# First queries over the two hardware DMA queues, and a score tile moved ahead of a token product, in a fused attention and mixer kernel

## The chip, the cores and the metric

One core of one Trainium2 chip. The time is that of the whole program on the device, in microseconds (us), as the median of several executions; lower is better. A profile is one of these executions with every instruction recorded.

## The reference

Attention with a squared ReLU, then a mixer over tokens and channels:

```python
scores = q @ k.transpose / sqrt(64)              # 8 batches, 12 heads, 448 tokens, 64 wide
attn = maximum(scores, 0) ** 2 / 448
x = attn @ v                                      # heads joined: (8, 448, 768)
h = maximum(x.T @ w_tok1, 0) @ w_tok2             # over tokens, 256 hidden
u = x + h.T
out = u + maximum(u @ w_ch1, 0) @ w_ch2           # over channels, 1536 hidden
```

Inputs and output are fp32; the kernel works in bf16 with fp32 sums.

## The kernel before

Work goes in steps of four heads (24 steps). The first keys come in fp32 over the two hardware queues (issued by the sync engine and by ScalarE) and are cast on chip; everything else is loaded by GpSimd, whose transfers cast on their way. PSUM is the memory into which PE, the matrix engine, writes its results; SBUF holds the operands. Tiles that the profile names: `xT` is a step's attention output, `x_sb` the same turned for the token product, `r_sb` the ReLU of a product, `uT` (`uT_sb`) the sum u.

```python
k_first = consts.tile([128, 2, QC, D], FP32, name="k_first")
def load_four(i, names="qkv"):
    for name in names:
        t = raw.tile([128, 2, QC, D], BF16, name=f"{name}_raw")
        for r in range(2):                                   # two heads on 64 partitions each
            eng, dst = nc.gpsimd, t
            if i == 0 and name == "k":
                eng, dst = (nc.sync, nc.scalar)[r], k_first
            eng.dma_start(...)
        if i == 0 and name == "k":
            nc.scalar.copy(t[:, 0], k_first[:, 0])           # the cast, half each
            nc.vector.tensor_copy(t[:, 1], k_first[:, 1])
        raws[i, name] = t
# ... (cut)
def transposes_first():
    for w, dst in ((1, keys), (0, queries)):                 # keys first
        # 28 matmuls that transpose raws[0, "qk"[w]] into PSUM (cut)
        if w:
            nc.scalar.copy(...); nc.vector.tensor_copy(...)  # keys to SBUF
        else:
            nc.vector.tensor_copy(...)                       # queries to SBUF
# ... (cut)
def scores(i, c, alone=False):
    ps = ps_att.tile([128, 2, 512], FP32, tag="att", name="sc_ps")   # two such buffers
    # 4 matmuls, then ReLU on ScalarE (on VectorE where alone); squares follow on VectorE (cut)
# ... (cut)
load_four(0, "kqv"); load_four(1, "qk"); load_wt1(); load_four(2, "qk")
load_four(1, "v"); load_wt2()
# ... (cut)
keep_clock(2, warm_ps)          # matmuls on zeros, whose result is not used
transposes_first()
keep_clock(3, warm_ps)
for i in range(DB):             # the first three steps
    for c in range(QC):         # seven score tiles
        scores(i, c, alone=(i, c) == (0, 2))
        # values, token products, transposes of the next step (cut)
        if c == 6:
            values(i, (0, 1))
            if i > 0:
                token1(i - 1)
```

Of the kernel before, what the change touches and what calls it, by code (L numbers as in the profile page):

```python
# [9 lines left out]
FP32 = mybir.dt.float32  # L10
# [6 lines left out]
def kernel(  # L17
# [11 lines left out]
    nc = tc.nc  # L29

    B, H, S, D = q.shape
# [7 lines left out]
    QC = S // 64  # L39
# [9 lines left out]
    consts = ctx.enter_context(tc.tile_pool(name="consts", bufs=1))  # L49
# [19 lines left out]


    raws = {}
    k_first = consts.tile([128, 2, QC, D], FP32, name="k_first")
    def load_four(i, names="qkv"):
        b, d = divmod(i, DB)
        for name in names:
            src = {"q": q, "k": k, "v": v}[name]
            t = raw.tile([128, 2, QC, D], BF16, name=f"{name}_raw")
            for r in range(2):
                h0 = 4 * d + 2 * r
                eng, dst = nc.gpsimd, t  # L80
                if i == 0 and name == "k":
                    eng, dst = (nc.sync, nc.scalar)[r], k_first
                eng.dma_start(  # L83
                    out=dst[64 * r : 64 * (r + 1)].rearrange("p g c d -> p g (c d)"),
                    in_=src[b, h0 : h0 + 2].rearrange("g (p c) d -> p g (c d)", c=QC),
                )
            if i == 0 and name == "k":
                nc.scalar.copy(t[:, 0], k_first[:, 0])
                nc.vector.tensor_copy(t[:, 1], k_first[:, 1])
            raws[i, name] = t  # L90

    def load_wt1():
        w = moe_w_tok1.rearrange("(p c) j -> c p j", c=QC)
        for c in range(QC):
            r = 64 * (c % 2)
            nc.gpsimd.dma_start(out=wt1[r : r + 64, c // 2, :], in_=w[c])
# [11 lines left out]
    def load_wc1(i, parts):  # L108
        n = DC // parts
        nc.gpsimd.dma_start(  # L110
            out=wc1[:, :, i * n : (i + 1) * n],
            in_=moe_w_ch1.rearrange("(g p) n -> p g n", p=128)[:, :, i * n : (i + 1) * n],
        )
# [44 lines left out]
    def transposes_first():  # L158

        sb = attn.tile([128, 2, 2, S], BF16, name="qkT")  # L160
        qkT[0] = sb
        keys = [ps_acc.tile([128, 1024], BF16, tag=f"acc{r}", name="kT_ps") for r in range(2)]
        queries = ps_att.tile([128, 2, 1024], BF16, tag="att", name="qT_ps")
        for w, dst in ((1, keys), (0, [queries[:, r] for r in range(2)])):
            for c in range(QC):
                for r in range(2):
                    h = slice(64 * r, 64 * (r + 1))
                    for g in range(2):
                        nc.tensor.matmul(
                            dst[r][64 * g : 64 * (g + 1), c * 64 : c * 64 + 64],  # L170
                            lhsT=raws[0, "qk"[w]][h, g, c, :],
                            rhs=ident[h, h],
                            is_transpose=True,
                            start=True,
                            stop=True,
                            skip_group_check=True,
                        )
            if w:
                nc.scalar.copy(sb[:, 0, 1], keys[0][:, :S])
                nc.vector.tensor_copy(sb[:, 1, 1], keys[1][:, :S])  # L180
            else:
                nc.vector.tensor_copy(sb[:, :, 0], queries[:, :, :S])

    def scores(i, c, alone=False):
        sb = qkT[i]
        ps = ps_att.tile([128, 2, 512], FP32, tag="att", name="sc_ps")
        for r in range(2):
            for g in range(2):
                h = slice(64 * g, 64 * (g + 1))
                nc.tensor.matmul(  # L190
                    ps[64 * r : 64 * (r + 1), g, :S],
                    lhsT=sb[h, r, 1, c * 64 : (c + 1) * 64],
                    rhs=sb[h, r, 0, :],
                    start=True,
                    stop=True,
                    skip_group_check=True,
                )
        at = attn.tile([128, 2, S], BF16, name="at", bufs=12)
        if alone:
            nc.vector.tensor_scalar(  # L200
                out=at, in0=ps[:, :, :S], scalar1=0.0, scalar2=None, op0=ALU.max
            )
        else:
            nc.scalar.activation(at, ps[:, :, :S], AF.Relu)  # L204
        squares.append(at)
        at2[i, c] = at

    def square(keep=0):
        while len(squares) > keep:
            at = squares.pop(0)  # L210
            nc.vector.tensor_tensor(out=at, in0=at, in1=at, op=ALU.mult)  # L211

    def values(i, cs):
        v_raw = raws[i, "v"]
        if i not in accs:
            accs[i] = [ps_acc.tile([128, 512], FP32, tag=f"acc{r}", name="acc_ps") for r in range(2)]
        ps = accs[i]
        for c in cs:
            at = at2.pop((i, c))
            for r in range(2):  # L220
                for g in range(2):
                    h = slice(64 * r, 64 * (r + 1))
                    nc.tensor.matmul(  # L223
                        ps[r][64 * g : 64 * (g + 1), :S],
                        lhsT=v_raw[h, g, c, :],
                        rhs=at[h, g, :],
                        start=(c == 0),
                        stop=(c == QC - 1),
                        skip_group_check=True,
                    )  # L230
# [58 lines left out]
    def token1(i):  # L289
        x_sb = x_tiles.pop(i)  # L290
        ps = ps_mm.tile([128, JC, 256], FP32, tag="bank", name="t1_ps")
        for j in range(JC):
            for c in range(4):
                nc.tensor.matmul(  # L294
                    ps[:, j, :],
                    lhsT=wt1[:, c, j * 128 : (j + 1) * 128],
                    rhs=x_sb[:, :, c, :],
                    start=(c == 0),
                    stop=(c == 3),
                )  # L300
        r1 = mix.tile([128, JC, 256], BF16, name="r1_sb")
        nc.scalar.activation(r1, ps, AF.Relu)
        r1_tiles[i] = r1
# [109 lines left out]
    def channel1_begin():  # L413
        r2_tiles[0] = mix.tile([128, EC, 2 * S], BF16, name="r2_sb")
        first = [ps_acc.tile([128, 512], FP32, tag=f"acc{e}", name="m1_ps2") for e in range(2)]
        for e in range(2):
            channel1_part(first, e, range(CC - 2))
        return first
# [122 lines left out]
    def keep_clock(n, warm_ps):  # L541

        for m in range(n):
            for r in range(2):
                h = slice(64 * r, 64 * (r + 1))
                nc.tensor.matmul(
                    warm_ps[h, :], lhsT=warm[h, :64], rhs=warm[h, :],
                    start=True, stop=True, skip_group_check=True,
                )
# [2 lines left out]
        nc.vector.memset(xT[i][:, :, S:], 0.0)  # L552
    nc.vector.memset(wt1[:, 3, :], 0.0)
    make_identity(nc, ident)
    load_four(0, "kqv")
    load_four(1, "qk")
    load_wt1()
    load_four(2, "qk")
# [10 lines left out]
    keep_clock(3, warm_ps)  # L569
    for i in range(DB):  # L570
        for c in range(QC):
            scores(i, c, alone=(i, c) == (0, 2))
            if i == 0:
                keep_clock(2 if c < 3 else c // 6, warm_ps)
            if i == 1 and c < 4:
                keep_clock(1, warm_ps)
            square(keep=1)
            if c < 3 and i > 0:
                values(i - 1, ((2, 3), (4, 5), (6,))[c])
                if c == 2:  # L580
                    values_out(i - 1, split=True)
            if c in (1, 2) and i > 1:
                token2(i - 2, early=True, rs=(c - 1,))
            if c == 3 and i == 0:
                transposes(1, "bank")
                warm_ps = ps_mm.tile([128, 512], FP32, tag="bank", name="warm_ps")
            if c == 4 and i > 0:
                x_back(i - 1, place="acc0", copy=nc.scalar.copy if i > 1 else None)
            if (i, c) in ((1, 3), (2, 5)):
                transposes(i + 1, "bank")  # L590
            if c == 6:
                values(i, (0, 1))
                if i > 0:
                    token1(i - 1)
        if i == 1:
            load_four(4)
        if i == 2:
            load_four(5)
            load_wc1(1, 2)


    i = DB
# [1 line left out]
    square()  # L604
    values(i - 1, (6,))
    values_out(i - 1, split=True)
    scores(i, 0)
    token2(i - 2, early=True, between=lambda: x_back(DB - 1, place="acc0"))
    scores(i, 1)
    token1(i - 1)  # L610
# [2 lines left out]
    first = channel1_begin()  # L613
# [118 lines left out]
```

## Time and profile before

| | before |
|---|---|
| median of the first three executions | 376.19 us (375.92 to 376.37) |
| span in the profile | 374.7 us |
| PE (matrix engine) busy | 365.0 us, 97% |
| first scores start in the profile | 8.03 us |
| last wait of PE over 0.2 us ends at | 32.28 us |

In the profile, DVE is VectorE, ACT is ScalarE, POOL is GpSimd and SP the sync engine; "L190" is a line of the kernel. A line of a waits view says who waited for whom, how long in total, how often, and the longest. A line of the slices view has one digit for each fortieth of the span. The one for the granted clock of PE, in tenths of full speed, is all nines before:

```profile
PEclk9999999999999999999999999999999999999999
```

### The profile page before, as it was taken

Reading aid. Unit: us, or ns where it says so; the run is one execution under the profiler, and the core shown is the slowest. Engines: PE = TensorE matmul, PEld = TensorE weight load, DVE = VectorE, ACT = ScalarE, POOL = GpSimd, SP = SyncE. Lnnn points to the kernel's source line nnn. Section 1 sums busy time; section 2 is a strip of 40 time slices with the busy share of each in tenths; the row PEclk is TensorE's granted clock in tenths of the full one; section 3 lists DMA queues with packets and bytes.
Section 4 is the critical chain, followed back from the end, with each engine's and each line's share of the span. In section 5 each row is a group of like instructions: output and inputs, shape, how many; then the busy total and the mean of one; then the engine's idle time right before and its main releaser. Section 6 shows DMA issues by size and latency. Waiting matters only on the chain.

```text
span 374.7 us, 10236 instructions
## 1 busy us (share of the span) xinstructions
PE 365.0 (97%) x4377; PEld 201.2 (54%) x4377; DVE 212.1 (57%) x414; ACT 211.0 (56%) x313; POOL 99.1 (26%) x185
## 2 busy tenths in 40 slices
PE   7889999999999999999999999999999999999996
PEld 3544555455555655565455655555555654555554
DVE  2986688756576666475554684575555755131022
ACT  3987888776345468725775457752775456311400
POOL 8956348304212403430330304412210000000000
PEclk9999999999999999999999999999999999999999
DMA  8999999923998886756765877758560534233024
GB/s 150 118 197 163 179 206 172 180 39 67 128 174 171 159 146 95 115 104 154 97 101 90 117 141 132 108 80 158 107 99 13 93 87 98 58 69 87 0 54 116
DMA packets 69566, 43.32 MB, mean 116 GB/s; under 512 B 43473, under 2 KB 66065, under 8 KB 69521
## 3 DMA queue, kind: packets, MB, share of 16 engines
q0 software_dynamic: 24496, 21.49, 40.8%
q1 hardware_dynamic: 44640, 20.75, 26.6%
q8 instruction: 34, 0.56, 0.6%
q10 hardware_dynamic: 384, 0.43, 0.4%
q14 instruction: 12, 0.09, 0.1%
HBM read 43.42 MB, written 11.01 MB: 145 GB/s over the span
## 4 chain that ended last, share of the span: by engine, by line
PE 89%; DVE 6%; ACT 1%; DMA 1%; issue 1%; POOL 0%; ACTq 0%; POOLq 0%; DVEq 0%
PE m_ps L443 29%; PE m_ps L404 28%; PE acc_ps L223 9%; PE sc_ps L190 9%; PE h_ps L353 4%; PE t_ps L312 3%; DVE at L211 2%; PE qkT_ps L140 2%; PE t_ps L294 1%; DMA q_raw<-in_q_dram 1%; DVE uT_sb L363 1%; PE t_ps L328 1%; ACT at L204 1%; DVE qkT L154 1%; PE x_ps L276 1%
## 5 line engine op out<-in xcount | busy, mean ns | idle before, releaser
L204 ACT ACTIVATE at<-sc_ps 128x896 bf16<-128x896 f32 x167 | 144.8, 924 | 49.7 <-PE sc_ps L190 49.7
L211 DVE TENSOR_TENSOR at<-at 128x896 bf16<-128x896 bf16 x168 | 97.7, 619 | 55.9 <-ACT at L204 55.9
L404 PE MATMUL m_ps<-uT_sb,wc 128*128 128x448 bf16 x564 | 115.5, 353 | 0.2 <-DVE uT_sb L363 0.2
L443 PE MATMUL m_ps<-wc,r_sb 128*128 128x384 bf16 x660 | 113.2, 326 | 0.0
L443 PEld LDWEIGHTS <-r_sb 128*128 128x128 bf16 x660 | 62.7, 98 | 46.7 <-issue 6.1
L411 ACT ACTIVATE r_sb<-m_ps 128x448 bf16<-128x448 f32 x94 | 51.3, 546 | 56.0 <-PE m_ps L404 55.6
L404 PEld LDWEIGHTS <-wc 128*128 128x128 bf16 x564 | 52.3, 98 | 53.4 <-issue 8.3
L450 DVE TENSOR_TENSOR out_sb<-m_ps,u_sb 128x384 f32<-128x384 f32 x55 | 30.5, 554 | 48.1 <-PE m_ps L443 48.1
L190 PE MATMUL sc_ps<-qkT 64*64 64x448 bf16 x672 | 53.2, 358 | 1.1 <-ACT at L204 0.9
L223 PE MATMUL acc_ps<-at,v_raw 64*64 64x448 bf16 x672 | 40.7, 351 | 1.5 <-DVE x_sb L285 0.7
L241 DVE TENSOR_SCALAR xT<-acc_ps 128x448 bf16<-128x448 f32 x45 | 26.1, 620 | 27.6 <-PE acc_ps L223 27.6
L659 POOL COPY gate<-x_sb 1x1 bf16<-1x1 bf16 x12 | 3.1, 254 | 126.9 <-DMA x_sb<-xT 126.9
L83 POOL DMA_DIRECT2D q_raw<-in_q_dram x48 | 28.9, 614 | 19.9 <-DMA wc<-in_moe_w_ch_dram 17.4
L363 DVE TENSOR_TENSOR uT_sb<-h_ps,xT 128x448 bf16<-128x448 f32 x48 | 27.7, 616 | 9.4 <-PE h_ps L353 9.3
L83 POOL DMA_DIRECT2D v_raw<-in_v_dram x48 | 29.6, 643 | 8.1 <-DMA wc<-in_moe_w_ch_dram 4.7
L338 ACT ACTIVATE r_sb<-t_ps 128x256 bf16<-128x256 f32 x36 | 11.8, 381 | 32.7 <-PE t_ps L328 28.5
L223 PEld LDWEIGHTS <-v_raw 64*64 64x64 bf16 x672 | 21.4, 106 | 15.7 <-issue 5.7
L190 PEld LDWEIGHTS <-qkT 64*64 64x64 bf16 x672 | 17.6, 105 | 21.9 <-issue 19.0
L83 POOL DMA_DIRECT2D k_raw<-in_k_dram x46 | 28.2, 634 | 1.7 <-issue 1.7
L154 DVE COPY qkT<-qkT_ps 128x896 bf16<-128x896 bf16 x44 | 25.3, 616 | 5.4 <-PE qkT_ps L140 5.4
L353 PE MATMUL h_ps<-wt,r_sb 128*128 128x448 bf16 x96 | 22.3, 353 | 0.0
L312 PE MATMUL t_ps<-x_sb,wt 128*128 128x256 bf16 x108 | 14.7, 273 | 0.0
(58 smaller groups left out, 150.7 us busy)
## 6 DMA issues: line engine op xcount, KB each, us to landing
out_dram<-out_sb SPq DMA_DIRECT2D x54, 192.0 KB, 2.9
q_raw<-in_q_dram POOLq DMA_DIRECT2D x48, 112.0 KB, 3.9
v_raw<-in_v_dram POOLq DMA_DIRECT2D x48, 112.0 KB, 4.8
k_raw<-in_k_dram POOLq DMA_DIRECT2D x46, 112.0 KB, 4.4
wc<-in_moe_w_ch_dram POOLq DMA_DIRECT2D x4, 1152.0 KB, 12.2
u_sb<-uT_sb SPq DMA_TRANSPOSE x48, 2.6
x_sb<-xT SPq DMA_TRANSPOSE x16, 3.2
k_first<-in_k_dram SPq DMA_DIRECT2D x1, 224.0 KB, 3.5
```

Source lines behind the costliest of these rows:

```text
L83: eng.dma_start(out=dst[64 * r : 64 * (r + 1)].rearrange("p g c d -> p g (c d)"), in_=src[b, h0 : h0 + 2].rearrange("g (p c) d -> p g (c d ...
L154: (nc.scalar.copy if split and r == 0 else nc.vector.tensor_copy)(sb[:, r].rearrange("n w t -> n (w t)"), parts[r][:, : 2 * S])
L190: nc.tensor.matmul(ps[64 * r : 64 * (r + 1), g, :S], lhsT=sb[h, r, 1, c * 64 : (c + 1) * 64], rhs=sb[h, r, 0, :], start=True, stop=True, s ...
L204: nc.scalar.activation(at, ps[:, :, :S], AF.Relu)
L211: nc.vector.tensor_tensor(out=at, in0=at, in1=at, op=ALU.mult)
L223: nc.tensor.matmul(ps[r][64 * g : 64 * (g + 1), :S], lhsT=v_raw[h, g, c, :], rhs=at[h, g, :], start=(c == 0), stop=(c == QC - 1), skip_gro ...
L353: nc.tensor.matmul(parts[r][:, :S], lhsT=r1[:, j, r * 128 : (r + 1) * 128], rhs=wt2[:, j, :], start=(j == 0), stop=(j == JC - 1),)
L363: nc.vector.tensor_tensor(out=uT_tiles[b // 2][:, 2 * d + r, off : off + S].rearrange("n (c p) -> n c p", c=QC), in0=parts[r][:, :S].rearr ...
L404: nc.tensor.matmul(ps[:, :S], lhsT=wc1[:, g, e * 128 : (e + 1) * 128], rhs=uT[:, g, off : off + S], start=(g == 0), stop=(g == CC - 1),)
L411: nc.scalar.activation(r2[:, e, off : off + S], ps[:, :S], AF.Relu)
L443: nc.tensor.matmul(ps[:, :HN], lhsT=r2[:, e, t * 128 : (t + 1) * 128], rhs=wc2[:, e, cols], start=(e == 0), stop=(e == EC - 1),)
L450: nc.vector.tensor_tensor(out=o[:, cols].rearrange("n (g d) -> n g d", d=128), in0=ps[:, :HN].rearrange("n (g d) -> n g d", d=128), in1=u_ ...
```

## The change

Its intent: the first scores wait for the first queries, so these take the way of the keys; and a ScalarE that waits for a token product gets a score tile first.

```diff
-            if i == 0 and name == "k":
-                eng, dst = (nc.sync, nc.scalar)[r], k_first
+            if i == 0 and name in first:                    # first = {"k": tile, "q": tile}
+                eng, dst = (nc.sync, nc.scalar)[r], first[name]
...
+    def cast_first(name):
+        t = raws[0, name]
+        nc.scalar.copy(t[:, 0], first[name][:, 0])
+        nc.vector.tensor_copy(t[:, 1], first[name][:, 1])
...
             if w:
+                cast_first("q")
                 nc.scalar.copy(sb[:, 0, 1], keys[0][:, :S])
                 nc.vector.tensor_copy(sb[:, 1, 1], keys[1][:, :S])
...
-    load_four(0, "kqv")
+    load_four(0, "kq")
+    cast_first("k")
+    load_four(0, "v")
...
-            scores(i, c, alone=(i, c) == (0, 2))
+            if c or i < 2:
+                scores(i, c, alone=(i, c) == (0, 2))
...
                 values(i, (0, 1))
                 if i > 0:
+                    scores(i + 1, 0)
+                    square(keep=1)
                     token1(i - 1)
...
-    scores(i, 0)                                            # step 3, after the loop
```

Below, "part A" is the queries' way and "part B" the moved tile.

## The prediction

> **What bounds the kernel now.** I read the page first: who is busy. Its first section says the matrix engine (PE) is busy for 365.0 of 374.7 us.
>
> ```profile
> PE 365.0 (97%) x4377; PEld 201.2 (54%) x4377; DVE 212.1 (57%) x414; ACT 211.0 (56%) x313; POOL 99.1 (26%) x185
> ```
>
> So at most 9.7 us can be won without taking PE work away, and the change takes none away: PE has 8756 rows before and after in the instruction order. Next I asked for the busy time of each engine by stretch (columns: stretch, its length, then busy us of PE, PEld, DVE, ACT, POOL with counts, granted clock, DMA share, GB/s).
>
> ```profile
> 5.00:10.00 5.00, 3.92 (x90) 2.14 (x87) 2.00 (x5) 2.64 (x4) 4.25 (x9) 1.00 1.17 170
> 10.00:15.00 5.00, 4.37 (x113) 2.57 (x113) 5.00 (x10) 4.52 (x7) 4.66 (x9) 1.00 0.77 92
> 15.00:20.00 5.00, 3.89 (x104) 2.13 (x99) 5.00 (x10) 5.00 (x7) 4.76 (x8) 1.00 1.14 161
> 25.00:35.00 10.00, 9.00 (x148) 5.32 (x148) 7.92 (x14) 8.18 (x11) 5.13 (x10) 1.00 1.13 182
> 45.00:55.00 10.00, 10.00 (x176) 5.69 (x176) 8.09 (x15) 8.44 (x13) 4.17 (x7) 1.00 1.20 204
> ```
>
> The kernel has three parts. Up to about 9 us it waits for the first data. From 10 to 20 us VectorE (DVE) is busy 5.00 of 5.00 us and ScalarE (ACT) nearly so: they bound it, and PE idles or runs filler matmuls. From about 37 us PE is busy throughout. Hence a microsecond won before 20 us moves all that follows, one for one; what is won there cannot exceed the few idle microseconds of PE. The change touches only the first 33 us. The chain of work that ended last (start us, us, what) shows which item sets each stretch:
>
> ```profile
> 2.15 4.70 DMA q_raw<-in_q_dram
> 6.84 0.04 issue
> 6.89 0.43 PE qT_ps L169 x26
> 7.33 0.02 issue
> 7.35 0.64 DVE qkT L182
> 7.99 0.04 issue
> 8.03 0.41 PE sc_ps L190 x4
> ```
>
> The first scores stand on the first queries: landed at 6.85, transposed, copied, scores at 8.03, which is 1.18 us after landing. Afterwards the chain goes through DVE without a gap from 9.41 to 19.65. The waits of PE after 9 us are few: 0.9 us (three) for score buffers that ACT still reads, 0.7 for the x_sb copy on DVE (at 19.70), 0.3 for DVE's xT at 25.01, 0.5 for ACT's x_sb copy at 27.32, 0.5 for DVE's x_sb copy at 32.28, 0.2 and 0.2 for the uT sums.
>
> **What the Trainium skill says.** (1) "DMA: Bandwidth & Descriptors", section "Issuing engines are not separate DMA queues": transfers started from sync, scalar or gpsimd run on the same 16 engines and interleave; more issuers save only issue time. The trace agrees that the engines are the scarce thing: their share is 0.9 to 1.4 in every half microsecond from 3 to 7 us. (2) The same page, "Anatomy of one DMA": a fixed cost of some 2 us per transfer, most of it the confirmation of the last write. Here the ACT half of the keys sent its last packets in 4.0 to 4.5 us and landed at 5.08 (issued at 1.18, landing 3.9 later), so about 0.8 us after its data. (3) "ScalarE: Activation LUTs", "What ACT_TABLE_LOAD costs": 186 ns plus 0.833 ns per element for an instruction with immediate operands, 559 ns for 448 elements. The key cast took 566 ns. (4) "TensorE: Matmul & The Clock Gate", "Architectural detail": weight loads may be pulled ahead, but ACT and DVE are strict first in, first out. So an instruction's place in the program decides here; no row of the trace runs out of that order.
>
> **The change, part by part.**
>
> Part A, queries. Removed: two GpSimd transfers (q of step 0), 0.63 us of issue each, 1.3 us of POOL; all its later loads move up by that. Added: one transfer behind each key transfer on the two hardware queues, and two casts. The cast costs are read off the key casts and the queues' progress off the DMA view in half microseconds (3.0 to 3.5, 3.5 to 4.0 and 4.5 to 5.0; columns: packets, MB, share of 16 engines):
>
> ```profile
> 5.20 0.57 ACT L88 CAST k_raw<-k_first 128x448 bf16<-128x448 f32 x1 [2.96 <-DMA k_first<-in_k_dram]
> 5.21 0.40 DVE L89 CAST k_raw<-k_first 128x448 bf16<-128x448 f32 x1 [3.52 <-DMA k_first<-in_k_dram]
> ...
> q1 hardware_dynamic: 68, 0.10, 51.5%
> q10 hardware_dynamic: 47, 0.08, 49.2%
> ...
> q10 hardware_dynamic: 71, 0.12, 94.0%
> q0 software_dynamic: 12, 0.01, 13.8%
> ...
> q0 software_dynamic: 102, 0.08, 139.2%
> ```
>
> Path after landing: the present 1.18 us, plus 0.57 (the slower cast, on ACT) plus some 0.09 of hand-over: 1.85 us. The key copies now stand behind the query cast, but 0.53 (ACT) and 0.39 (DVE) fit beside the 0.43 us of transposes. So A wins only if q lands before 8.03 - 1.85 = 6.18 us, that is 0.67 earlier than today.
>
> When does it land? The two key transfers are 144 packets each; 77 of those 288 had gone by 3.0 us. With q there are 576, so 499 remain at 3.0. The two hardware queues together moved 115 packets in a half microsecond, 230 per us: 207 go by 3.9, when the software queue starts, leaving 292. That queue now carries v instead of q and is always full. I assume (an estimate) that the three queues take equal turns: a hardware packet is 70 ns of one engine (0.5 x 16 / 115), a software one about 109 (1.39 x 0.5 x 16 / 102), so a turn of 249 ns gives 16 x 2 / 0.249 = 129 hardware packets per us, and 292 take 2.3 us: data end at 6.2. The 139% says that packets overlap within an engine, so I shorten this to 5.8. With 0.8 us of confirmation q lands at 6.6, scores start at 6.6 + 1.85 = 8.45 in place of 8.03: A costs about **0.4 us**. The q transfer on the sync queue also competes with the key half on the ACT queue, so key casts start perhaps 0.3 us later; that lies beside the wait for q.
>
> Part B, the moved score tile, for steps 1 to 2 and 2 to 3. It removes nothing. ACT idles 1.12 us at 21.29 waiting for token product 0 (8 matmuls, 0.99 us). With scores(2,0) ahead, PE runs it at 20.27 to 20.58, ACT's relu fills that hole (20.6 to 21.5) rather than running at 21.78, and the token relu is done near 22.25, still before PE wants it (22.44 now, 22.55 then). PE has no wait between 19.70 and 24.75, so it gains nothing there. DVE does: its square at 22.72 moves into its 1.48 us of idle time, uT starts at 23.0 instead of 23.27, xT ends 0.2 earlier and PE's 0.26 us wait at 25.01 nearly goes; the 0.5 at 27.32 follows ACT, which is 0.15 to 0.2 ahead. Gain: 0.2 us. The second place is mixed: DVE gets one more square (0.53 us) ahead of xT, where it idled 0.47 for PE, and the token relu now stands behind another relu, so the next token product waits 0.1 to 0.3 us, against the 0.31 us of scores no longer in that stretch: gain 0.1. Sum of B: **-0.3 us**.
>
> Sum: 376.19 + 0.4 - 0.3 = 376.3; I take 376.2, as the turns among the queues may favour the two hardware queues.
>
> **The rivals.** (a) The hardware queues win their turns: data of q end at 5.2 (499 / 230 after 3.0), landing 6.0, scores 7.85, A gains 0.2, total 375.7. For it: while the keys were moving, queue 0 moved only 12 packets in 3.5 to 4.0; against it: that may only be its start. (b) The software queue takes half of the turns and v delays q to 7.0 or more: A costs 0.8 to 1.0, total 376.8. (c) The wait for q was hidden anyway: against it, the chain runs through it, and DVE has no gap from 9.41 to 19.65. (d) The second moved tile makes a new wait, the token relu or xT behind the extra square, and B gives back 0.3. The excess GpSimd time gains nothing in any of these: PE waited 0.5 us at most for later loads.
>
> **Range and chances.** A lies between -0.3 and +0.9, B between -0.6 and +0.1, and the three runs spread 0.45. All lie within 0.3% of 376: faster or slower by 2% would need 7.5 us, more than all of PE's waits. So **376.2 us**, range 375.5 to 376.9, chances 0.01, 0.985, 0.005.
>
> **What would show it.** A: the landing of q_first (right at 6.4 to 6.8), both q casts of 0.57 and 0.40 us, and the start of the first scores at 8.3 to 8.6; wrong if scores start before 8.0. B: ACT's idle time before the token relu at 21 us gone, PE's wait for xT at 25 us under 0.1; wrong if PE waits for r_sb or xT near 30 us by more than 0.3. From 37 us on all must run as before, shifted. The number is wrong if a later stretch changes PE's waits, or if DVE is no longer without gaps from the first square to 19.65.

## The result, and the profile after

381.15 us (380.90 to 381.58, four runs) against 376.12 of the kernel before: ratio 1.0135, 95% interval 1.0117 to 1.0152. A ratio here is the mean time of one kernel's fast runs over that of the other's from the same rounds, so not quite the ratio of the medians. The forecast was 376.2 with a range to 376.9, so it was wrong by 5 us.

The lines of the page, and the busy times of the same stretches as before (stretch, length, busy us of PE, PEld, DVE, ACT, POOL, granted clock, DMA share, GB/s):

```profile
PE 367.3 (97%) x4377; PEld 202.1 (53%) x4377; DVE 212.9 (56%) x415; ACT 211.9 (56%) x314; POOL 97.7 (26%) x183
PEclk9799999999999999999999999999999999999999
```

```profile
5.00:10.00 5.00, 1.88 (x65) 1.02 (x66) 1.27 (x4) 1.56 (x3) 2.86 (x7) 0.83 1.13 194
10.00:15.00 5.00, 5.00 (x48) 2.40 (x46) 2.14 (x4) 1.83 (x2) 4.83 (x9) 0.50 0.79 91
15.00:20.00 5.00, 4.24 (x116) 2.66 (x109) 4.92 (x10) 4.85 (x7) 4.87 (x8) 0.99 1.11 162
```

Two things strike. From 5 to 10 us PE is busy only 1.88 us (3.92 before), and from 10 to 15 us the granted clock is 0.50: PE is "busy" for all 5.00 us there with 48 matmuls, where the kernel before had 113. DVE, which had no idle time from 10 us, is busy 2.14 of 5. The chain of work that ended last shows the start:

```profile
1.94 6.54 DMA q_first<-in_q_dram
...
8.56 0.57 ACT q_raw L93
9.13 0.04 issue
9.18 0.59 PE qT_ps L174 x14
9.77 1.28 PE warm_ps L552 x6
11.04 0.41 PE sc_ps L196 x6
```

and the waits of PE:

```profile
PE qT_ps L174 <- ACT q_raw L93: 2.9, 1, 2.9
```

The queries landed at 8.48 us, not earlier than before (6.85) but 1.63 later, and not at the 6.6 of the prediction. After the cast and the transposes, filler matmuls at half speed (six of them take 1.47 us from the first start to the last end, 0.84 before) stand in the chain. Three marks in both traces put numbers on it: the first scores start at 8.03 before and 10.50 after (+2.47); the first value matmuls of step 1 at 19.70 and 24.10 (+4.40); the wait of PE for the uT sums at 37.29 and 42.07 (+4.78). At 68.27 and 73.05 the distance is still 4.78. So the loss is made in three stretches, 2.47 + 1.93 + 0.38, and everything after 42 us runs as before, shifted. The span grew by 5.1; the remaining 0.3 is in the later part and the tail.

One trace stands for the kernel before here, and its start is a late one. In three traces told below with the same program for the start (b_only, b_first, b_tr4) the queries landed at 6.20 to 6.23 us and the first scores started at 7.64, 7.38 and 7.41. The value matmuls of step 1 still started at 19.68, 19.23 and 19.89, so most of the earlier start was gone by then; PE waited 0.3 to 0.9 us for the keys of step 2, near 17 us. The first two stretches together (4.40) are thus known to about half a microsecond, and their division less well.

### The profile page after: what moved, and what is told of

Its sections match the earlier page's. It is cut to its first block, busy times and chain, and to the rows that moved or that the text cites. A ratio compares the mean times of both kernels' runs of the same rounds, so it can differ in the third digit from the quotient of the medians.

```text
span 379.8 us, 10240 instructions
## 1 busy us (share of the span) xinstructions
PE 367.3 (97%) x4377; PEld 202.1 (53%) x4377; DVE 212.9 (56%) x415; ACT 211.9 (56%) x314; POOL 97.7 (26%) x183
## 4 chain that ended last, share of the span: by engine, by line
PE 88%; DVE 4%; ACT 3%; DMA 3%; issue 1%; ACTq 0%; SPq 0%; DVEq 0%
PE m_ps L449 29%; PE m_ps L410 27%; PE sc_ps L196 9%; PE acc_ps L229 9%; PE h_ps L359 4%; PE t_ps L318 3%; PE qkT_ps L145 2%; ACT at L210 2%; DMA q_first<-in_q_dram 2%; PE t_ps L300 1%; DMA x_sb<-xT 1%; PE t_ps L334 1%; DVE at L217 1%; PE warm_ps L552 1%; DVE uT_sb L369 1%
## 5 line engine op out<-in xcount | busy, mean ns | idle before, releaser
L196 PE MATMUL sc_ps<-qkT 64*64 64x448 bf16 x672 | 55.0, 363 | 1.7 <-ACT at L210 1.6
L85 POOL DMA_DIRECT2D q_raw<-in_q_dram x46 | 27.6, 612 | 17.8 <-DMA wc<-in_moe_w_ch_dram 15.0
```

The costliest lines, as they stand in the source:

```text
L85: eng.dma_start(out=dst[64 * r : 64 * (r + 1)].rearrange("p g c d -> p g (c d)"), in_=src[b, h0 : h0 + 2].rearrange("g (p c) d -> p g (c d ...
L196: nc.tensor.matmul(ps[64 * r : 64 * (r + 1), g, :S], lhsT=sb[h, r, 1, c * 64 : (c + 1) * 64], rhs=sb[h, r, 0, :], start=True, stop=True, s ...
```

## The experiments

My theory: the late queries cost 2.5 us; the long wait they cause makes the chip halve PE's clock, which costs another 1 to 2; the moved tile costs 0.4. Rivals: the moved tile costs much more; the clock is a symptom that costs nothing; the queries are late for a reason other than what runs beside them.

**a_only**: part A without part B (the loop as in the kernel before).

> The query part alone (the score tile stays where it was before). Theory (the late landing of the queries and the half clock that follows the long PE wait cost it all): q_first lands near 8.4 us, PE waits 2.9 us, the granted clock is near 0.5 from 10 to 15 us, and the time is 380.5 to 381.5, all of the change's +5.0 within 0.5. Rival (the moved score tile costs a good part): 378 to 380.

Measured 380.25 us, ratio 1.0111 (1.0098 to 1.0125): +4.1, somewhat less than the theory's 4.5 and more than the rival allows. First scores at 10.48. Here the half clock lasted from 10.02 to 13.43 us, one window of 3.41 us; in the changed kernel from 8.26 to 15.08, two of them. Both lengths occur: over the whole span the mean clock is 0.991 in three of four runs of the changed kernel and 0.995 in one; of part A alone it is 0.995 in three and 0.991 in one. In the first of the changed kernel's two windows PE had 2.49 us of work; in the six profiled runs with one such window it had 2.77 to 3.41. That this decides the length was not tested.

**b_only**: part B on the kernel before.

> The moved score tile alone, on the kernel before. The prediction's step: 375.9 (-0.3). Theory after the result: PE's waits near 32 us in the changed kernel (0.25 us for ACT before the moved scores) say it gains nothing: 376.0 to 376.6. The clock stays at 1.00 in both. Rival (the moved tile costs much): over 377.

Measured 376.57 us, ratio 1.0008 (0.9995 to 1.0022): unclear by the total time, +0.45 in the medians. The trace is sharper. From the first value matmuls of step 1 to the wait for the uT sums it takes 37.29 - 19.70 = 17.59 us before, 37.65 - 19.68 = 17.97 here, and 42.07 - 24.10 = 17.97 in the changed kernel. The distance repeats well: the six other traces without part B and with full clock in this stretch (a_only, a_fill, a_gate, swap, v_hold, reord) give 17.59 or 17.60, and full_fill, with part B, 17.98. So part B costs 0.38 us; the forecast gain of 0.3 is refuted. What its trace shows at the second place (PE rows; in brackets the idle time before and who ended it):

```profile
27.26 0.57 PE L223 MATMUL acc_ps<-at,v_raw 64*64 64x448 bf16 x8 [0.52 <-ACT x_sb L285]
28.09 0.38 PE L190 MATMUL sc_ps<-qkT 64*64 64x448 bf16 x4 [0.25 <-DVE qkT L154]
```

The moved scores themselves make PE wait 0.25 us.

**a_fill**: part A alone with filler matmuls that keep PE at work while the queries are under way.

```diff
             if w:
+                keep_clock(12, warm_ps)     # 24 matmuls on zeros
                 cast_first("q")
```

> The query part alone with 24 filler matmuls in the program between the key and the query transposes, some 2.6 us at full clock, so that PE is not idle while the queries are on their way. Theory (half of the loss is the clock): the granted clock stays at 1.00, the first scores start near 10.1, the relu row of ACT starts 2.0 us earlier than in the changed kernel, total 378.3 to 379.2. Rival (the clock is a symptom and costs nothing, as DVE and ACT bound this stretch): 380.5 to 381.5.

Measured 378.97 us, ratio 1.0074 (1.006 to 1.0087). The same microsecond in a_only (first line) and here (second; only PE's busy time, clock, DMA share and GB/s):

```profile
10.00:11.00 1.00, 1.00 (x12) 0.51 0.68 79
```

```profile
10.00:11.00 1.00, 0.91 (x14) 1.00 0.68 72
```

The first scores start at 10.48 and 10.47, so the filler delays nothing. From there to the value matmuls of step 1 it takes 23.31 - 10.48 = 12.83 us in a_only and 22.14 - 10.47 = 11.67 here, exactly as before (19.70 - 8.03 = 11.67). One window of half clock therefore costs 1.2 us, and the two of the changed kernel 24.10 - 10.50 - 11.67 = 1.9. Adding 24 useless matmuls made it 1.28 us faster than a_only. The rival is refuted.

**full_fill**: the same filler in the whole change.

> The whole change with the 24 filler matmuls between key and query transposes. Theory (the three costs add up: later start 2.5, half clock, moved tile 0.4): with the clock at 1.00 it lands at the time of the query part with filler (378.97) plus that of the moved tile (0.45): 379.2 to 379.6. Rival (the moved tile costs more when the start is late, as the whole change was 0.9 over the query part alone): 379.7 or more.

Measured 379.31 us, ratio 1.0088 (1.0074 to 1.0102). The costs add up: a_fill and b_only together give 376.12 + 2.85 + 0.45 = 379.42. The difference from the changed kernel, 1.84 us, is the price of the clock there.

**a_gate**: part A, with GpSimd held back by a copy of one column of the landed queries.

```diff
+    gq = consts.tile([128, 1], BF16, name="gq")
+    nc.gpsimd.tensor_copy(gq, first["q"][:, 1, QC - 1, D - 1 :])
     load_four(0, "v")
```

> The query part alone, with all loads of GpSimd held back by a one-element copy that reads the landed queries, so that the two hardware queues have the DMA engines to themselves. Theory 1 (packets of the software queue push the queries back): q_first lands at 6.0 to 6.6. Theory 2 (a second transfer on a hardware queue starts late by itself, its packets began 2.4 and 3.1 us after issue): it lands at 7.2 or later. In both the loads of step 1 come later, so the total says little: 378 to 382.

Measured 381.97 us, ratio 1.0157, which says little, as the loads of step 1 come later. The landing lies between the two theories:

```profile
1.92 4.86 DMA q_first<-in_q_dram
```

That is 6.8 us. In the four traces of part A with all loads running they landed at 8.48 to 8.73. What ran beside the queries thus cost them 8.48 - 6.8 = 1.7 us. Yet even with the DMA engines to themselves they are no earlier than the queries of the kernel before (6.85 in its trace, 6.20 to 6.23 in the three others). The first scores start at 8.63. The DMA view from 4.5 to 5.0 us (packets, MB, share of 16 engines; q1 is the sync engine's hardware queue, q10 ScalarE's, q0 GpSimd's software queue) in a_gate and in the changed kernel:

```profile
q1 hardware_dynamic: 56, 0.08, 67.6%
q10 hardware_dynamic: 27, 0.05, 42.1%
```

```profile
q1 hardware_dynamic: 55, 0.10, 65.9%
q0 software_dynamic: 41, 0.03, 35.6%
q10 hardware_dynamic: 6, 0.01, 6.7%
```

Each transfer is 144 packets. Counted in order on its queue, the second transfer's first packet ran at 3.72 us on q1 and 4.27 on q10 in a_gate, 0.33 and 0.12 us after the last of the keys, though both were issued before 2 us; in the changed kernel at 3.87 and 4.63 (0.37 and 0.23 after). So it begins when the keys ahead of it are out, and then runs slower than the prediction reckoned: from 4 to 6 us the two queues moved 278 packets in a_gate and 207 in the changed kernel, that is 139 and 104 per us where 230 was the rate taken from the keys. The tail of the changed kernel, 6.5 to 7.0 us:

```profile
q0 software_dynamic: 91, 0.07, 91.8%
q10 hardware_dynamic: 20, 0.03, 21.6%
q1 hardware_dynamic: 3, 0.00, 2.5%
```

q10 still has packets of the queries, and goes on with 18 and 7 in the next two half microseconds, while q0 moves 100 and 119. The half clock in a_gate came later, from 15.11 us, after PE had waited for step 1's queries and keys.

**swap**: part A with the queries ahead of the keys on both hardware queues (the names in the load call turned round).

> The query part alone with the order on the two hardware queues turned round: queries first, keys behind them. One look. Theory (the late one is whichever transfer stands second on the hardware queues, as those two queues feed one transfer after another): queries land near 5.1 us, keys near 8.4. Rival (something about the queries' data, or the cast, is slow): queries still land after 7. Total as the query part alone, within 1 us of 380.3.

Measured once: 380.19 us. The queries (first line, us from issue to landing, least, median, most) and the keys (second) change places. Of the keys' two transfers the view has the landing of one only, on the sync engine's queue; their cast, which needs both, starts at 8.4:

```profile
DMA to landing us min/median/max: 3.4/3.7/4.0
```

```profile
DMA to landing us min/median/max: 5.6/5.6/5.6
```

So it is the second place on the queue that is late, whatever it holds.

**v_hold**: the kernel before, with all that follows its first queries held back until the keys have landed.

> The kernel before with the loads behind the first queries (v of step 0 and all later ones) held back until the keys have landed. Theory (what runs beside the queries pushes their landing back): q lands by 6.2 instead of 6.85. Rival (the landing is set by when its descriptors are ready, not by the traffic beside): 6.7 to 6.9. The total may rise by the later loads of step 1: 375.8 to 377.5.

Measured 380.22 us, ratio 1.0116, above the expected range. The queries landed at 5.91, as the theory has it (query transposes at 6.20 us without a wait), and the first scores started at 7.44. That is no earlier than 7.38 and 7.41 in b_first and b_tr4, where nothing was held. The held loads of step 1 then made PE wait 1.8 us for queries near 11.6 us, and the granted clock went to 0.50 from 14.84 on. The gain was far outweighed.

**q_early**: the kernel before with its first two query loads ahead of the identity matrix on GpSimd.

> The kernel before with GpSimd issuing the first queries ahead of making the identity matrix, 0.7 us earlier. Theory (the first scores stand on the landing of the queries, and what is won there comes through to the end): q lands near 6.2 instead of 6.85, scores start at 7.5 to 7.8 instead of 8.03, total 375.6 to 375.9. Rival (the software queue then takes turns from the keys, which land later by as much): keys cast at 5.5 or later, total 376.0 to 376.4.

Measured 376.54 us (375.84 to 378.19), ratio 1.0012 (0.9999 to 1.0026): no gain. Both sides were partly right: the query transposes did not wait (the queries landed at 5.92), the first scores started at 7.82, within the 7.38 to 8.03 that the unchanged start shows, but the keys were cast only at 5.71 instead of 5.20. The 378.19 is the profiled run, in which the clock was halved from 19.96 us.

**reord** and **reord_delay**: GpSimd's loads in the order of their use; the second with a pause behind the first queries.

```diff
-    load_four(0, "kqv")
-    load_four(1, "qk")
-    load_wt1()
-    load_four(2, "qk")
+    load_four(0, "kq")
+    # reord_delay: nc.gpsimd.memset(pause, 0.0), a tile of 128 x 1280
+    load_four(1, "qk")
+    load_four(0, "v")
+    load_four(2, "qk")
+    load_wt1()
```

> The kernel before with GpSimd's loads in the order of their use: q and k of step 1 ahead of v of step 0, q and k of step 2 ahead of the seven small loads of the first token weights. Theory (after the first scores it is the late key loads of step 2, waited for 0.3 to 0.7 us near 17 us in several traces, that keep a good start from coming through): no wait for k_raw in the trace, 375.5 to 375.9. Rival (ACT and DVE bound this stretch whatever the loads do): 376.0 to 376.3.

> The same order of loads, with a pause of about 1.2 us (a memset of an unused tile) on GpSimd behind the first queries, so that the next loads do not run beside them. Theory (the queries land at 6.0 to 6.2 when nothing follows at once, and step 1's loads are then no later than in the kernel before): first scores at 7.4 to 7.6 in every trace, total 375.3 to 375.8. Rival (the paused loads are waited for in step 1): a wait for q_raw or k_raw near 10 to 12 us and 376.2 or more.

reord: 375.83 us (375.60 to 375.97) against 376.03, ratio 0.9993 (0.9979 to 1.0007). No matmul waits for k_raw in the trace, as expected, but none did in the kernel before's own trace either, and the gain is not clear of the noise. reord_delay: 376.01 us (375.69 to 378.37), ratio 1.001 (0.9989 to 1.003): nothing, and again one run, the profiled one, with a half clock (from 20.77 us). So no version here is shown to beat the kernel before.

**b_first**: part B at the first place only.

> The moved score tile at the first place only (step 1 to 2), on the kernel before. Theory (the second place costs it all, by the wait of the moved scores for the copy of their own queries, 0.25 us, and 0.3 us more PE work ahead of the values): 376.0 to 376.2, and in the trace PE waits for the uT sums near 37.2 us as in the kernel before (37.29), not near 37.65. Rival (both places cost alike): 376.3 and 37.45 us.

Measured 376.04 us (375.73 to 376.88) against 376.03. In the trace 36.79 - 19.23 = 17.56 us, 0.03 less than the 17.59 of before. The first place is neutral and the second costs 0.41. (The absolute mark, 36.79, is earlier than expected because the start of this run was earlier, first scores at 7.38. A profile of the same start can differ by some tenths, so I compare distances.)

**b_tr4**: part B, with step 3's transposes and their copies one score tile earlier.

```diff
-            if (i, c) in ((1, 3), (2, 5)):
+            if (i, c) in ((1, 3), (2, 4)):
                 transposes(i + 1, "bank")
```

> The moved score tile alone (both places), with the transposes and copies of step 3's queries and keys one score tile earlier, so that the tile moved at the second place need not wait for the copy of its own queries. Measured inside the trace, from the start of the value matmuls of step 1 (19.7 us) to PE's wait for the uT sums (37.3 us): 17.59 in the kernel before, 17.97 with the moved tile, 17.56 with the first place only. Theory (0.25 us of the second place's 0.41 is that wait): the wait of scores for the query copy is gone and the distance is 17.7 to 17.8. Rival (PE then waits as long for ACT, whose relus fill the same two buffers): 17.9 to 18.0. Total 376.0 to 376.6 either way.

Measured 376.86 us against 376.47, ratio 1.0018 (0.9997 to 1.0039), and 37.86 - 19.89 = 17.97 us. My theory fell. The wait is as long and has another name:

```profile
28.30 0.38 PE L190 MATMUL sc_ps<-qkT 64*64 64x448 bf16 x4 [0.25 <-ACT at L204]
```

The third score tile in a row needs one of two buffers, and ACT is still at their ReLUs. In b_only the ReLU that freed the buffer ended at 27.98 and the copy at 28.03 us, so the copy that the profile named was only the later of two.

**When the clock halves.** The changes of the granted clock lie on a grid of 3.41 us, placed differently in each run. I asked the traces for PE's busy time in these windows. In seven the next window ran at half clock; the fullest of them, in reord_delay, and what followed it:

```profile
17.36:20.77 3.41, 2.19 (x22) 1.00 1.08 141
20.77:24.18 3.41, 3.41 (x31) 0.50 1.16 173
```

The work in the seven was 0.56 (swap), 0.68 (a_only), 1.00 (a_gate), 1.22 (changed kernel, from 4.84 to 8.25 us), 1.70 (v_hold), 1.88 (q_early) and 2.19. No sharp line divides them from the rest, for the clock stayed full after two windows with less work than the last of these, one of a_gate and one of v_hold:

```profile
4.87:8.28 3.41, 2.00 (x67) 1.00 0.28 64
8.01:11.43 3.42, 2.02 (x21) 1.00 1.03 137
```

In all the other full-clock windows of the fourteen traces, from the first record of the clock (4 to 7 us) to 39 us, PE had at least 2.23 us of work, and the clock stayed. In the kernel before the emptiest had 2.41. So in these runs the clock fell after every window with 1.88 us or less, after none with 2.23 or more, and between them both happened. Which of PE's work is counted was not tested; leaving out the transposes draws no line either (the a_gate window then has 1.35 us, that of reord_delay 2.14).

## Why the prediction was wrong

The start was to lose 0.4 us, the clock nothing, and part B to win 0.3. Measured at the three marks: 2.47, 1.93 and 0.38 lost. So steps of the mechanism failed, not only a size.

- **"With 0.8 us of confirmation q lands at 6.6."** (Confirmation is the time from a transfer's last data to its landing.) It landed at 8.48. The failed step is the estimate that the two hardware queues go on at 230 packets per us until 3.9 and then take two turns of three, so that all packets are out by 5.8. In the changed kernel they moved 162 packets in 3 to 4 us, 207 in 4 to 6 and still 94 in 6 to 8. Nor did the software queue take a steady share: it moved 13 packets in 5 to 6 us and 354 in 6 to 8. In a_gate, without a software queue, the second transfers still landed at 6.8 and swap shows that whichever stands second is late; what runs beside cost a further 1.7. Rival (b), "v delays q to 7.0 or more", had the direction; its cost of 0.8 to 1.0 is less than half of the 2.47. The 1.85 us path after landing was right: at full clock the first scores follow the landing by 1.85 in a_fill (8.62 to 10.47) and a_gate (6.78 to 8.63). The casts took 0.57 and 0.39; the 559 ns beside the first in the prediction is an estimate from the page's formula. The break-even of 6.18 us was not tested, as no run of part A came near it.
- **A step that was missing.** The prediction read the clock column (1.00 throughout) and took it as given. PE's idle time was treated as free until 20 us. A wait of 2.9 us left 1.22 us of work in a 3.41 us window, and the clock was halved for 3.4 or 6.8 us: 1.2 to 1.9 us, measured by a_only, a_fill and full_fill. The fillers in the code, and the Trainium skill's "TensorE: Matmul & The Clock Gate", Part 1, by which PE's clock is at half after an idle window of about 3.4 us, were both on the table.
- **"Gain: 0.2 us", first place of B.** It was 0.03. PE's wait for xT did go, but 0.17 us of it came back as a wait of the next scores for ACT (at 25.55 us in b_only). The DVE half of the argument was right; ACT, busy without a gap from 24.15 to 29.65 us in b_only, kept the rest.
- **"Gain 0.1", second place of B.** It cost 0.41. The waits named there (token ReLU behind another ReLU, xT behind the extra square) did not appear as waits of PE; the one that did is that of the moved scores for a buffer, 0.25 us. Their own 0.31 us of PE work now stands ahead of the values, and only part of it, judging by the marks in the trace, was won back later. The sum of B was +0.38 where -0.3 stood.
- **"... a microsecond won before 20 us moves all that follows, one for one."** What is lost does come through (2.44 of 2.44 us in a_fill, from the first scores to the uT sums). What is won need not: starts 0.39, 0.65 and 0.62 us earlier (b_only, b_first, b_tr4) left the value matmuls of step 1 earlier by 0.02 and 0.47 and later by 0.19. The chain without a gap in the one trace did not show the loads of step 2, for whose keys PE waited in these three.
- **Right:** from 42 us on (37 before) all ran as before, but for some 0.3 us at the end; PE's work is the same (4377 matmuls and 4377 weight loads on both pages; the prediction's 8756 stands on neither); 0.57 + 0.40 for the casts; B on its own is within the noise of the total.

Open: why the second transfers' packets run so much more slowly than the keys' did, even with nothing beside them, and why ScalarE's queue sends so few beside the software queue at the end. The trace shows when packets ran, not what they waited for.

## What to carry to other kernels

Moving a transfer to another queue moves its place in that queue: look up what stands ahead of it and what will take its old place, and find the landing time that breaks even before trusting the move. When a change lengthens a wait of PE, count PE's work in each 3.4 us window, because a wait can halve the clock of the next 3.4 or 6.8 us; filler matmuls were cheap insurance here. A tile issued ahead needs a free buffer at that moment, so count the buffers and the engine that drains them, not only the idle time that it is to fill.

## What the Trainium skill lacked or had wrong

- "TensorE: Matmul & The Clock Gate", Part 1, says that the clock falls after at least one idle window of about 3.4 us. The grid of 3.41 us agrees. But here PE need not be idle for a window: it fell after windows with 1.22 us of work (changed kernel) and even 2.19 us (reord_delay), and stayed after 2.00 (a_gate). In the changed kernel it fell at 8.26 us, 2.0 us after PE's last matmul. The page gives no busy share.
- "DMA: Bandwidth & Descriptors", "Issuing engines are not separate DMA queues", says that several issuers save only issue time. Where a transfer stands matters more here: first on a hardware queue it landed 3.4 to 4.2 us after issue in the runs of part A, second 4.9 us with nothing beside it (a_gate) and up to 6.8 with the software queue at work (full_fill). The page gives no times for that.
- The same page's table of first-byte latencies (about 0.6 us for hardware, 1 us for software queues) does not say from when they count. Here the first key packet ran at 2.28 us, 1.5 after the sync engine's issue began and 0.8 after it ended; the first software packet ran at 3.65 us, 2.2 and 1.5 after.
